# A list scheduler inside the kernel, loads per block of 128 tokens, and one transfer queue

## The chip, the cores and the metric

One core of a Trainium2 chip. The metric is the time of one execution on the device in microseconds, median of the runs in the fast state. Ratios are the mean time of one kernel's fast runs over that of the other's of the same rounds, so they are not quite the ratios of the medians quoted. Spans and times inside an execution come from a profiled run, whose span is 1.7 to 1.9 us shorter than that run's own time.

## The reference

Two stages. The first is a gated linear attention (4 batches, 8 heads, 768 tokens, head size 48), the second a feed-forward layer over 3072 tokens of width 384 with 2048 hidden units:

```python
f = 1 / (1 + exp(-f_logit))
for t in range(S):                                     # per batch and head
    state = f[t][:, None] * state + outer(k[t], v[t])  # 48 x 48
    y[t]  = q[t] @ state
x = y as (3072, 384)
h = x @ w_in                                           # 384 x 2048
out = softplus(h) @ w_out                              # 2048 x 384
```

## The kernel before

The tokens are cut into 24 blocks of 128. For each block the attention turns the recurrence into matmuls (cumulated log gates `cs`, transposes `qkT`, scores `pp`, state `uu`, output `oo`, transpose back `xTp`). The feed-forward layer is `f1` (48 matmuls a block into `hh`, then exp and log on ScalarE) and `f2` (16 matmuls a block into `ops`). A fixed plan sets the order: attention of a block runs 40 steps ahead of its first `f1`, and `f2` 30 steps behind `f1`.

```python
    def load(name, t, b, hold=False):                   # one batch (6 blocks) of one tensor
        sb = work.tile([128, H, NC, 64], FP32, name=name, tag=name, bufs=2)
        ...
        nc.sync.dma_start(out=sb.rearrange("p h c d -> p (h c) d")[:, :, 0:D],
                          in_=t[b].rearrange("h (c p) d -> p (h c) d", p=T))
    load("ff", f_logit, 0); load("kk", k, 0); load("qq", q, 0); load("vv", v, 0)   # (cut)
    ...
    def load_w_in(w):                                   # GpSimd's queue, cast to bf16 by the DMA
        nc.gpsimd.dma_start(out=w_in_bf[:, :, w * WQ:(w + 1) * WQ], in_=...)
    ...
    for s in range(min(plan), NS + LAG):
        if 0 <= s < NS:
            f1(*divmod(s, NJ))
        for fn, a in plan.get(s, []):                   # attention pieces and loads of this step
            fn(*a)
        if 0 <= s - LAG < NS:
            f2(*divmod(s - LAG, NJ))
```

Of the kernel before, what the change touches and what calls it, by code (L numbers as in the profile page):

```python
# [15 lines left out]
LAG = 30  # L16
LEAD = 40


@with_exitstack  # L20
def kernel(
# [27 lines left out]
    in_t = {}  # L49

    def load(name, t, b, hold=False):
        sb = work.tile([128, H, NC, 64], FP32, name=name, tag=name, bufs=2)
        if hold:
            nc.vector.memset(sb[0:1, 0, 0, 0:1], 0.0)
        nc.sync.dma_start(  # L55
            out=sb.rearrange("p h c d -> p (h c) d")[:, :, 0:D],
            in_=t[b].rearrange("h (c p) d -> p (h c) d", p=T))
        in_t[name, b] = sb

    load("ff", f_logit, 0)  # L60
    load("kk", k, 0)
    load("qq", q, 0)
    load("vv", v, 0)

# [30 lines left out]
    WQ = 512  # L95

    def load_w_in(w):
        nc.gpsimd.dma_start(
            out=w_in_bf[:, :, w * WQ:(w + 1) * WQ],
            in_=moe_w_in[:, w * WQ:(w + 1) * WQ].rearrange("(r p) n -> p r n", p=128))  # L100

    def load_w_out(w):
        nc.gpsimd.dma_start(  # L103
            out=w_out_bf[:, 4 * w:4 * w + 4, :],
            in_=moe_w_out[512 * w:512 * (w + 1), :].rearrange("(j p) n -> p j n", p=128))
# [6 lines left out]
    def emit_bias(w):  # L112
        if w == 0:
            bias_ps[0] = att_bank("biasps")
        for j in range(4 * w, 4 * w + 4):
            nc.tensor.matmul(out=bias_ps[0][:, 0:DM], lhsT=ones, rhs=w_out_bf[:, j, :],
                             start=(j == 0), stop=(j == NJ - 1), skip_group_check=True)
        if w == 3:
            nc.vector.tensor_scalar(out=bias_bc, in0=bias_ps[0][:, 0:DM], scalar1=LN2,
                                    scalar2=None, op0=ALU.mult)  # L120
# [4 lines left out]
    def a_z(i):  # L125
        b, c = divmod(i, NC)
        ft = in_t["ff", b][:, :, c:c + 2, 0:D]
        zt = work.tile([128, 2, H, D], BF16, name="zz", tag="zz", bufs=2)
        nc.scalar.activation(out=ft, in_=ft, func=AF.Exp, bias=0.0, scale=-1.0)  # L129
        nc.scalar.activation(out=zt.rearrange("p c h d -> p h c d"), in_=ft, func=AF.Ln,  # L130
                             bias=1.0, scale=1.0)
        z_t[i], z_t[i + 1] = zt[:, 0], zt[:, 1]

    def a_cs(i):
        ps = att_bank("cs")
        nc.tensor.matmul(out=ps[:, 0:DM], lhsT=negU, rhs=z_t.pop(i).rearrange("p h d -> p (h d)"),  # L136
                         start=True, stop=True, skip_group_check=True)
        cs_ps[i] = ps

    def a_e(i):  # L140
        ps = cs_ps.pop(i)[:, 0:DM].rearrange("p (h d) -> p h d", h=H)
        et = e_bufs[i % 2]
        nc.scalar.activation(out=et[:, H:2 * H, 0:D], in_=ps, func=AF.Exp, bias=0.0, scale=-1.0)  # L143
        nc.scalar.activation(out=et[:, 0:H, 0:D], in_=ps, func=AF.Exp, bias=0.0, scale=1.0)

    def a_mul(i):
        b, c = divmod(i, NC)
        et = e_bufs[i % 2]
        qkp = qkp_bufs[i % 3]
        k_eng = nc.vector if i == 0 else nc.gpsimd  # L150
        k_eng.tensor_tensor(out=qkp[:, H:2 * H, 0:D], in0=in_t["kk", b][:, :, c, 0:D],  # L151
                            in1=et[:, H:2 * H, 0:D], op=ALU.mult)
        nc.gpsimd.tensor_tensor(out=qkp[:, 0:H, 0:D], in0=in_t["qq", b][:, :, c, 0:D],  # L153
                                in1=et[:, 0:H, 0:D], op=ALU.mult)
        if i == 0:
            for w in range(4):
                load_w_in(w)
        vb = work.tile([128, DM], BF16, name="vb", tag="vb", bufs=3)
        nc.gpsimd.tensor_copy(out=vb.rearrange("p (h d) -> p h d", h=H),  # L159
                              in_=in_t["vv", b][:, :, c, 0:D])  # L160
        vb_t[i] = vb
        if i == 1:
            for w in range(4):
                load_w_out(w)

    def a_tr(i):
        qkp = qkp_bufs[i % 3].rearrange("p (a b) d -> p a (b d)", b=2)
        ps = att_bank("qkT", BF16, 1024)
        for a in list(range(NP, 2 * NP)) + list(range(NP)):
            nc.tensor.transpose(ps[:, a * 128:(a + 1) * 128], qkp[:, a, :], ident)  # L170
        qkT = work.tile([128, 2 * NP, 128], BF16, name="qkT", tag="qkT", bufs=2)
        qbd = qbd_bufs[i % 2]
        pv = ps.rearrange("p (a t) -> p a t", t=128)
# [5 lines left out]
    def a_p(i):  # L179
        qkT = qkT_t[i]  # L180
        qbd = qbd_bufs[i % 2]
        pt = work.tile([128, H, 128], BF16, name="ptm", tag="ptm", bufs=2)
        for half in range(2):
            ps = att_bank("pp")
            for u in range(2):
                p = 2 * half + u
                nc.tensor.matmul(out=ps[:, u * 256:(u + 1) * 256], lhsT=qkT[0:112, NP + p, :],  # L187
                                 rhs=qbd[0:112, p, :], start=True, stop=True,
                                 skip_group_check=True)
            nc.vector.tensor_tensor(out=pt[:, 4 * half:4 * half + 4, :],  # L190
                                    in0=ps.rearrange("p (a t) -> p a t", t=128), in1=mask4,
                                    op=ALU.mult)
        ptm_t[i] = pt

    def a_u(i):
        c = i % NC
        if c == NC - 1:
            return
        qkp = qkp_bufs[i % 3].rearrange("p (a b) d -> p a (b d)", b=2)
        ek = e_bufs[i % 2].rearrange("p (a b) d -> p a (b d)", b=2)  # L200
        vb = vb_t[i]
        ps = att_bank("uu")
        for p in range(NP):
            nc.tensor.matmul(out=ps[:, 96 * p:96 * p + 96], lhsT=qkp[:, NP + p, :],  # L204
                             rhs=vb[:, 96 * p:96 * p + 96], start=True, stop=True,
                             skip_group_check=True)
# [3 lines left out]
        so, sn = s_bufs[i % 2], s_bufs[(i + 1) % 2]  # L210
# [3 lines left out]
        nc.vector.tensor_copy(out=ec, in_=ps[:, DM:DM + NP])  # L214
        for lo, e0 in ((0, 0), (64, D)):
            hi = lo + 48
            if c == 0:
                nc.vector.tensor_copy(out=tt[lo:hi], in_=uu[lo:hi, :, e0:e0 + D])
            else:
                nc.vector.tensor_tensor(out=tt[lo:hi], in0=uu[lo:hi, :, e0:e0 + D],  # L220
                                        in1=so[lo:hi, :, e0:e0 + D], op=ALU.add)
        for lo, e0 in ((0, 0), (64, D)):
# [5 lines left out]
    def a_o(i):  # L228
        c = i % NC
# [3 lines left out]
        if c > 0:  # L233
# [11 lines left out]
        xt = work.tile([128, DM], BF16, name="xx", tag="xx", bufs=2)  # L245
        nc.vector.tensor_copy(out=xt, in_=ps[:, 0:DM])  # L246
        x_t[i] = xt

    def a_xt(i):
# [4 lines left out]
        xT = work.tile([128, KT, T], BF16, name="xT", tag="xT", bufs=3)  # L254
        nc.vector.tensor_copy(out=xT, in_=ps[:, 0:DM].rearrange("p (r t) -> p r t", r=KT))
        xT_t[i] = xT


    h_ps, u_t, g_t, o_ps = {}, {}, {}, {}

    def f1(i, j):
        if j == 0:
            g_t[i] = work.tile([128, NJ, T], BF16, name="gg", tag="gg", bufs=4)
        if j % 4 == 0:
            h_ps[0] = psum.tile([128, 4, T], FP32, name="hh", tag="hh", bufs=2)
        if j % 8 == 0:
            u_t[0] = work.tile([128, 8, T], FP32, name="uexp", tag="uexp", bufs=3)
        hp = h_ps[0]
        xT = xT_t[i]
        for r in range(KT):  # L270
            nc.tensor.matmul(out=hp[:, j % 4, :], lhsT=w_in_bf[:, r, j * 128:(j + 1) * 128],  # L271
                             rhs=xT[:, r, :], start=(r == 0), stop=(r == KT - 1),
                             skip_group_check=True)
        if j % 4 == 3:
            a = j % 8 - 3
            nc.scalar.activation(out=u_t[0][:, a:a + 4, :], in_=hp, func=AF.Exp, bias=0.0,  # L276
                                 scale=1.0)
        if j % 8 == 7:
            nc.scalar.activation(out=g_t[i][:, j - 7:j + 1, :], in_=u_t[0], func=AF.Ln,  # L279
                                 bias=0.5, scale=0.5)  # L280

    def f2(i, j):
        if j == 0:
            o_ps[i] = psum.tile([128, 512], FP32, name="ops", tag="ops", bufs=2)
        ps = o_ps[i]
        nc.tensor.matmul(out=ps[:, 0:DM], lhsT=g_t[i][:, j, :], rhs=w_out_bf[:, j, :],  # L286
                         start=(j == 0), stop=(j == NJ - 1), skip_group_check=True)
        if j == NJ - 1:
            osb = work.tile([128, DM], FP32, name="osb", tag="osb", bufs=4)
            nc.vector.tensor_tensor(out=osb, in0=ps[:, 0:DM], in1=bias_bc, op=ALU.add)  # L290
            nc.sync.dma_start(out=out[i * T:(i + 1) * T, :], in_=osb)


    plan = {}

    def at(s, fn, *a):
        plan.setdefault(s, []).append((fn, a))

    for i in range(NB):
        s0 = NJ * i - LEAD  # L300
        if i % 2 == 0:
            at(s0 - 4, a_z, i)
        at(s0, a_cs, i)
        at(s0, a_e, i)
        at(s0 + 2, a_mul, i)
        at(s0 + 10, a_tr, i)
        at(s0 + 12, a_u, i)
        at(s0 + 17, a_p, i)
        at(s0 + 23, a_o, i)
        at(s0 + 27, a_xt, i)  # L310
    for b in range(1, B):
        s0 = 4 if b == 1 else NJ * (NC * (b - 1) - 1) - LEAD + 4
        at(s0, load, "ff", f_logit, b, b == 1)
        at(s0 + 1, load, "kk", k, b)
        at(s0 + 2, load, "qq", q, b)
# [41 lines left out]
```

## Time and profile before

| | before |
|---|---|
| time, median | 231.3 us (fast runs 231.27, 231.50 and, timed later with the changed kernel, 230.50; one slow run of 295.32 left out). The prediction works with 231.5, the figure known when it was written |
| span of the profiled run | 228.5 us (that run took 230.25) |
| TensorE (PE) busy | 182.9 us, 80% |
| ScalarE (ACT), VectorE (DVE), GpSimd (POOL) busy | 63%, 53%, 35% |
| first f1 matmul | 41.5 us |

The busy shares are averages over a start that waits for transfers and a body that TensorE fills. The lines that show the two are in the prediction, with how to read them.

### The profile page before, as it was taken

The numbers are of one execution on the slowest core, as the hardware profiler recorded it, in microseconds if no ns is written. First come the engines' busy times: TensorE is split into PE (matmuls) and PEld (weight loads), VectorE is DVE, ScalarE is ACT, GpSimd is POOL, SyncE is SP. The second block draws the span as 40 slices with busy tenths as digits, with TensorE's granted clock in tenths as the row PEclk, the third lists the DMA queues.
The fourth block names the chain that finished last, engine by engine and source line by source line (L and its number), as shares of the span: only waits on it lengthen the run. The fifth ranks groups of instructions, "written<-read, shape, count | busy, mean of one in ns | idle before, by whom it ended". The sixth has DMA issues, their size and how long they took to land.

```text
span 228.5 us, 5679 instructions
## 1 busy us (share of the span) xinstructions
PE 182.9 (80%) x2368; PEld 148.3 (65%) x2368; DVE 120.3 (53%) x270; ACT 143.3 (63%) x217; POOL 80.2 (35%) x127
## 2 busy tenths in 40 slices
PE   0001127888999299999999999999999999999994
PEld 0000014775887177887778878888788787888872
DVE  7100217665664346664856667666567576665011
ACT  2130014197688069689687897887968879677760
POOL 1000529655133051455223543445143552440000
PEclk9999999999999979999999999999999999999999
DMA  5999999999999999999599799200011000110101
GB/s 111 163 164 163 163 185 167 201 174 168 150 176 166 167 165 168 190 164 214 126 165 158 154 165 185 98 34 35 3 37 39 34 4 34 39 39 34 37 34 69
DMA packets 32026, 27.10 MB, mean 119 GB/s; under 512 B 768, under 2 KB 32000, under 8 KB 32000
## 3 DMA queue, kind: packets, MB, share of 16 engines
q1 hardware_dynamic: 28288, 23.60, 58.9%
q0 software_dynamic: 3712, 3.15, 9.1%
q8 instruction: 18, 0.29, 0.6%
q14 instruction: 8, 0.07, 0.1%
HBM read 25.17 MB, written 4.72 MB: 131 GB/s over the span
## 4 chain that ended last, share of the span: by engine, by line
PE 52%; DMA 19%; SPq 13%; ACT 7%; POOL 4%; DVE 2%; issue 1%; DVEq 0%; POOLq 0%
PE ops L286 21%; PE hh L271 19%; DMA vv<-in_v_dram 14%; SPq L55 13%; DMA out_dram<-osb 5%; PE pp L187 3%; PE qkT L170 3%; ACT zz L130 3%; ACT ff L129 2%; ACT uexp L276 2%; PE cs L136 2%; PE oo L241 1%; POOL w_out_bf L103 1%; PE oo L236 1%; PE uu L204 1%
## 5 line engine op out<-in xcount | busy, mean ns | idle before, releaser
L271 PE MATMUL hh<-xT,w_in_bf 128*128 128x128 bf16 x1152 | 125.6, 221 | 0.5 <-ACT uexp L276 0.5
L286 PE MATMUL ops<-w_out_bf,gg 128*128 128x384 bf16 x384 | 121.1, 328 | 0.0
L271 PEld LDWEIGHTS <-w_in_bf 128*128 128x128 bf16 x1152 | 95.9, 99 | 26.3 <-issue 1.6
L276 ACT ACTIVATE uexp<-hh 128x512 f32<-128x512 f32 x96 | 57.0, 595 | 44.4 <-PE hh L271 44.0
L279 ACT ACTIVATE gg<-uexp 128x1024 bf16<-128x1024 f32 x48 | 50.7, 1057 | 1.5
L190 DVE TENSOR_TENSOR ptm<-pp,mask 128x512 bf16<-128x512 f32 x48 | 30.9, 686 | 20.5 <-PE pp L187 20.4
L286 PEld LDWEIGHTS <-gg 128*128 128x128 bf16 x384 | 37.6, 98 | 5.8 <-issue 3.7
L224 POOL TENSOR_TENSOR sst<-tt,ec 48x192 bf16<-48x192 f32 x40 | 20.1, 503 | 55.1 <-DVE tt L220 45.3
L151 POOL TENSOR_TENSOR qkp<-kk,ee 128x384 bf16<-128x384 f32 x23 | 21.0, 913 | 35.5 <-ACT ee L143 35.3
L174 DVE COPY qkT<-qkT 128x1024 bf16<-128x1024 bf16 x24 | 16.6, 691 | 29.0 <-PE qkT L170 29.0
L153 POOL TENSOR_TENSOR qkp<-qq,ee 128x384 bf16<-128x384 f32 x24 | 21.9, 914 | 23.4 <-DMA qq<-in_q_dram 23.4
L170 PEld LDWEIGHTS <-qkp 128*128 128x128 bf16 x192 | 12.4, 102 | 25.8 <-DVE qkp L151 17.1
L170 PE MATMUL qkT<-ident,qkp 128*128 128x128 bf16 x192 | 16.6, 230 | 13.3 <-POOL qkp L153 7.5
L143 ACT ACTIVATE ee<-cs 128x384 bf16<-128x384 f32 x24 | 11.4, 475 | 22.8 <-PE cs L136 22.8
L290 DVE TENSOR_TENSOR osb<-ops,bias_bc 128x384 f32<-128x384 f32 x24 | 13.4, 558 | 22.2 <-PE ops L286 20.1
L136 PE MATMUL cs<-zz,negU 128*128 128x384 bf16 x24 | 8.5, 352 | 16.0 <-ACT zz L130 16.0
L246 DVE CAST xx<-oo 128x384 bf16<-128x384 f32 x24 | 13.4, 557 | 7.3 <-PE oo L241 6.9
L187 PE MATMUL pp<-qbd,qkT 112*128 112x256 bf16 x96 | 15.4, 284 | 0.5 <-DVE qbd L176 0.5
L129 ACT ACTIVATE ff<-ff 128x768 f32<-128x768 f32 x12 | 10.0, 836 | 8.6 <-DMA ff<-in_f_logit_dram 8.6
L204 PE MATMUL uu<-vb,qkp 128*128 128x96 bf16 x80 | 7.2, 217 | 10.3 <-POOL vb L159 10.3
L159 POOL CAST vb<-vv 128x384 bf16<-128x384 f32 x24 | 12.1, 503 | 8.6 <-DMA vv<-in_v_dram 8.6
L204 PEld LDWEIGHTS <-qkp 128*128 128x128 bf16 x80 | 5.3, 105 | 10.5 <-issue 10.5
(41 smaller groups left out, 149.5 us busy)
## 6 DMA issues: line engine op xcount, KB each, us to landing
out_dram<-osb SPq DMA_DIRECT2D x24, 192.0 KB, 2.3
w_in_bf<-in_moe_w_in_dram POOLq DMA_DIRECT2D x4, 384.0 KB, 9.0
w_out_bf<-in_moe_w_out_dram POOLq DMA_DIRECT2D x4, 384.0 KB, 7.0
ff<-in_f_logit_dram SPq DMA_DIRECT2D x4, 0.2 KB, 10.2
kk<-in_k_dram SPq DMA_DIRECT2D x4, 0.2 KB, 16.0
qq<-in_q_dram SPq DMA_DIRECT2D x4, 0.2 KB, 13.6
vv<-in_v_dram SPq DMA_DIRECT2D x4, 0.2 KB, 16.5
```

Of the source, the lines that this page charges most:

```text
L55: nc.sync.dma_start(out=sb.rearrange("p h c d -> p (h c) d")[:, :, 0:D], in_=t[b].rearrange("h (c p) d -> p (h c) d", p=T))
L151: k_eng.tensor_tensor(out=qkp[:, H:2 * H, 0:D], in0=in_t["kk", b][:, :, c, 0:D], in1=et[:, H:2 * H, 0:D], op=ALU.mult)
L153: nc.gpsimd.tensor_tensor(out=qkp[:, 0:H, 0:D], in0=in_t["qq", b][:, :, c, 0:D], in1=et[:, 0:H, 0:D], op=ALU.mult)
L170: nc.tensor.transpose(ps[:, a * 128:(a + 1) * 128], qkp[:, a, :], ident)
L174: nc.vector.tensor_copy(out=qkT, in_=pv)
L187: nc.tensor.matmul(out=ps[:, u * 256:(u + 1) * 256], lhsT=qkT[0:112, NP + p, :], rhs=qbd[0:112, p, :], start=True, stop=True, skip_group_c ...
L190: nc.vector.tensor_tensor(out=pt[:, 4 * half:4 * half + 4, :], in0=ps.rearrange("p (a t) -> p a t", t=128), in1=mask4, op=ALU.mult)
L224: nc.gpsimd.tensor_tensor(out=sn[lo:hi, :, e0:e0 + D], in0=tt[lo:hi], in1=ec[lo:hi].unsqueeze(2).to_broadcast([48, NP, D]), op=ALU.mult)
L271: nc.tensor.matmul(out=hp[:, j % 4, :], lhsT=w_in_bf[:, r, j * 128:(j + 1) * 128], rhs=xT[:, r, :], start=(r == 0), stop=(r == KT - 1), sk ...
L276: nc.scalar.activation(out=u_t[0][:, a:a + 4, :], in_=hp, func=AF.Exp, bias=0.0, scale=1.0)
L279: nc.scalar.activation(out=g_t[i][:, j - 7:j + 1, :], in_=u_t[0], func=AF.Ln, bias=0.5, scale=0.5)
L286: nc.tensor.matmul(out=ps[:, 0:DM], lhsT=g_t[i][:, j, :], rhs=w_out_bf[:, j, :], start=(j == 0), stop=(j == NJ - 1), skip_group_check=True)
```

## The change

Its intent: block 0 should not wait for a whole batch, the weights should not fight the loads for the DMA, and every engine should get its instructions in an order that a small simulation finds good. The kernel now builds a list of tasks with costs and needs, runs a list scheduler over it on the host, and emits the instructions in the order found. Cut to the core:

```diff
-    def load(name, t, b, hold=False):
-        sb = work.tile([128, H, NC, 64], FP32, name=name, tag=name, bufs=2)
+    def load(n, i):                                     # one block of one tensor
+        t = work.tile([128, H, D], FP32, name=n + n, tag=n + n, bufs=LOADS)      # LOADS = 4
...
-        nc.gpsimd.dma_start(out=w_in_bf[...], in_=moe_w_in[...])
+            t = work.tile([128, KT, WQ], FP32, name="w32", tag="w32", bufs=3)
+            nc.sync.dma_start(out=t, in_=moe_w_in[...])
+        eng = (nc.vector, nc.gpsimd)[a]                 # each casts one half
+        eng.tensor_copy(out=d[:, :, m * a:m * a + m], in_=t[:, :, m * a:m * a + m])
...
+def in_order(tasks, slots):
+    queue = {e: sorted((t for t in tasks if t.engine == e), key=lambda t: t.key) for e in clock}
+    def ready(t):                                       # needs, and the users of the buffer's last turn
+        ...
+    while len(order) < len(tasks):
+        # per engine: the first task by key that can start earliest; over all engines: the earliest
...
+    turn = (blocks(0, 1, 2, 3) + [("wi", w) for w in range(4)] + [("wo", w) for w in range(4)]
+            + blocks(*range(4, NB)))
+    for kd, (n, i) in enumerate(turn):
+        if n in SRC:
+            task(("go", n, i), "SP", 0.5, [(used[n], i - LOADS)], kd, load, (n, i))
+            task(("dma", n, i), "DMA", 1.15, [("go", n, i)], kd)
+            ...
+        else:
+            task(("go", n, i), "SP", 0.5, [], kd, load_w, (n, i), "w32", [("cast", n, i, 1)])
+            task(("dma", n, i), "DMA", 2.45, [("go", n, i)], kd)
+            ...
```

Attention, f1 and f2 keep their instructions; they are split into tasks (`z1`, `z2`, `tr`, `ev`, ...), the lag of f2 becomes 24, and there are more buffers for the block's result (`xT` 6) and the activations (`gg` 6).

## The prediction

> **What bounds the kernel now.** I read three views in this order: the page's 40 slices, the chain of work that ended last, and counts of one matmul line per stretch. The slices say where the time goes:
>
> ```profile
> PE   0001127888999299999999999999999999999994
> DMA  5999999999999999999599799200011000110101
> ```
>
> One slice is 5.7 us. TensorE (PE) does almost nothing for six slices (about 33 us), is near full from the tenth, has one hole (the 2 at slice 14), and is full to the end. The DMA engines are full from slice 2 to 25 and then nearly idle. So the kernel has two parts: a start that waits for transfers, and a body bound by TensorE. The chain names the transfers:
>
> ```profile
> 0.80 0.84 SPq L55
> ...
> 15.27 16.84 DMA vv<-in_v_dram
> 32.17 0.51 POOL vb L159
> ...
> 62.01 16.25 DMA vv<-in_v_dram
> 78.38 0.51 POOL vb L159
> 78.94 0.35 PE uu L204 x4
> ```
>
> Each load moves one whole batch (six blocks of 128 tokens) of one tensor. Block 0 needs only a sixth of each, but waits until v, the fourth, is there at 32.2 us. Batch 1 repeats it: v lands at 78.3. The matmuls in order of time show what that costs:
>
> ```profile
> 74.30 0.33 PE L271 MATMUL hh<-xT,w_in_bf 128*128 128x128 bf16 x3
> 78.94 0.35 PE L204 MATMUL uu<-vb,qkp 128*128 128x96 bf16 x4 [4.31 <-POOL vb L159]
> ...
> 79.23 0.48 PE L286 MATMUL ops<-w_out_bf,gg 128*128 128x384 bf16 x1
> 79.51 0.53 PE L271 MATMUL hh<-xT,w_in_bf 128*128 128x128 bf16 x3
> ```
>
> The bracket is the idle time before the group. TensorE stands for 4.3 us and comes back slower (0.53 us for three matmuls against 0.33).
>
> How fast is the body? Busy time does not say, because matmuls overlap. I count the first feed-forward matmuls (L271, 48 per block); columns are stretch, length, matmul busy (count), weight-load busy (count), clock, DMA share, GB/s:
>
> ```profile
> 41.50:60.00 18.50, 10.31 (x111) 8.18 (x111) 1.00 1.12 177
> 72.00:80.00 8.00, 2.14 (x18) 1.76 (x19) 0.95 1.09 166
> 100.00:120.00 20.00, 13.85 (x126) 10.42 (x126) 1.00 0.89 168
> 120.00:140.00 20.00, 14.60 (x134) 11.23 (x135) 1.00 0.97 160
> 140.00:160.00 20.00, 14.74 (x135) 11.11 (x134) 1.00 0.29 77
> ```
>
> At best 134.5 per 20 us, or 7.14 us a block. The chain's steps give the same: a step of three f1 matmuls and one f2 matmul is 0.33 us, 16 steps are 5.28, and attention adds cumsum 0.165, transposes 0.44, scores 0.43, state 0.28, output 0.38, transpose back 0.165 = 1.86. So TensorE's warm work is 24 x 7.14 + 16 bias matmuls x 0.165 = **174.0 us**. The last matmul ends at 225.1, so 51 us are lost: about 37 before the first f1 at 41.5 (only some 4.3 us of attention was done by then), 6 at the batch-1 hole (4.3 idle plus some 1.8 at half speed), 1.2 in 100 to 120, the other 6 to 7 in 41.5 to 60 (slow clock, and no f2 until w_out is there) and around 85. After the last matmul come 3.4 us (addition, store, end).
>
> **What the Trainium skill says.** "DMA: Bandwidth & Descriptors", section "Issuing engines are not separate DMA queues": transfers from all engines run on the same 16 DMA engines. The trace agrees: loads alone move 163 GB/s, and vv, issued at 15.3, waits for qq and lands at 32.2. Hence one queue costs no bandwidth, and the order is what counts. The same page, "Specifications", wants at least 512 B for full rate. The rows here are 192 B, and stay so on the DRAM side; 163 GB/s agrees. "TensorE: Matmul & The Clock Gate", "Part 1: The HAM clock gate": after a few idle us the array runs at half rate until it has been busy for some 3.4 us. The trace agrees (steps of 0.64 us after the hole, until 82.6). "SBUF — State Buffer", "SBUF: two separate sides": some VectorE copies and GpSimd hold one shared port pair exclusively. That bears on the new casts, done half by each engine; the kernel before has no such pair to show it.
>
> **The change, part by part.** All compute operations stay; the logistic part is cut per block (two of about 0.49 us for each block instead of two of 0.84 for two blocks: 24 x 0.98 - 12 x 1.68 = 3.4 us more on ScalarE, busy 143 of 228 now, so hidden). Added are 16 casts (8 of about 0.8 on VectorE, 8 of about 1.05 on GpSimd, the change's own costs), 6.4 and 8.4 us on engines at 53% and 35%. GpSimd loses 6.2 us of weight issues.
>
> 1. Loads per block. Batch loads land at 10.6, 17.9, 25.2 and 32.2: 7.27 us each, so 1.21 us for a sixth. The sixteen loads of blocks 0 to 3 use the DMA until 0.8 + 16 x 1.21 = 20.2 us; block 0 is complete near 7.5. Attention of four blocks (7.4 us warm, double cold) fits in before the weights.
>
> 2. Weights after them. From 32 to 38 us the trace shows some 205 GB/s, nearly all weights written as bf16, read from twice as many bytes, so a 0.79 MB piece took about 2 us to read; the change's scheduler assumes 2.45, since all bytes are now written too. I take 2.3. The first w_in quarter is moved at 22.5, lands about 1.8 later (the change's figure; a store measures 2.3 from issue to landing), and is cast in 1.05: first f1 at **25.3 us instead of 41.5**. The eight pieces are moved by 20.2 + 18.4 = 38.6, the last cast at 41.5.
>
> 3. Work done by 41.5: attention of four blocks 7.4, f1 of four blocks 4 x 2.64 = 10.6, three quarters of the f2 of block 0 (2.0) and of the bias (2.0): 22.0 us. Lost so far: **19.5 us**, against 37.
>
> 4. From 41.5 until block 4. Its q is moved at 38.6 + 3 x 1.21 = 42.2, lands at 44, and its chain (multiply 0.91, transpose 0.44, copies 1.53, scores and mask 1.5, output 0.38, copy 0.56, transpose 0.17, copy 0.36, seven handovers) takes about 6.3: f1 of block 4 at 50.3. In those 8.8 us TensorE has the rest of f2 for blocks 0 to 3 (8.6), of the bias (0.65) and attention of block 4 (1.86): 11.1 us. So it should stay dense. Thereafter a block takes 4.84 of loads and some 0.6 of store, less than 7.14, so the DMA runs ahead and the batch-1 hole vanishes. I allow 2 us idle in 41.5 to 60, 1 for clock changes, and 2 for places where the set order does not meet real times.
>
> 5. Sum: 174.0 + 19.5 + 2 + 1 + 2 = 198.5 for the last matmul, + 3.4 = 202 span. Before, the timed runs exceed the span by 3.0 us (231.5 against 228.5), the profiled one by 1.75; so **205 us**, a ratio of 0.885.
>
> **The rivals.** (a) The weights are paced by their buffers, not by the DMA. There are three 32-bit buffers for eight pieces; one turn is transfer 2.3 + landing 1.8 + cast 1.05 + issue and first byte about 1.5 = 6.7 us for three, 2.2 each: just on the edge. If the two casts block each other on the shared port (0.8 + 1.05 instead of 1.05), or stand behind attention work, it becomes 2.6 to 3 each and everything after step 2 shifts 3 to 6 us: 208 to 211. For it: the tight sum. Against it: VectorE and GpSimd have little else then.
>
> (b) TensorE starves after the weights: blocks 4 and on come one at a time at 4.84 us, with no stock, and the load of block i waits for the use of block i-4, stores standing in the same issue order behind it. For it: the store that took 10.8 us behind batch loads before. Against it: now at most a few 1.2 us loads lie ahead. It would leave holes in 45 to 65 and slow-clock stretches: 210 to 216.
>
> (c) The static order is wrong on the chip: an in-order engine waits for something the scheduler believed done, and ScalarE (6.06 us per block of 7.14, two PSUM banks between it and TensorE) passes each delay on. The body would run at 7.4 to 7.6 a block: 5 to 10 us more. Against it: the costs in the scheduler are those in the trace (0.165, 0.6, 1.06, 0.91).
>
> (d) The early gain is hidden. It is not, since after the start TensorE is the only bound and its lost time adds directly to the end.
>
> **Range and chances.** The best case (weights at 2 us, no allowances) is about 198; (a) and (b) together about 215. I say 205 us, 199 to 215 in 8 of 10. Faster by over 2% needs anything below 226.9; it would take losses as large as the whole gain to miss that: faster 0.95, same 0.03, slower 0.02.
>
> **What would show it.** In the new profile: f1 starts at 25 to 26 us; PE's slices show some work from the second slice and are near full from the eighth or ninth, without the 2; the four loads of a block land 1.2 us apart; w_out is cast by 41 to 43 us; the L271-like matmul goes at 134 per 20 us from 60 us on; PE's last matmul is at 196 to 202. Wrong would be: a first f1 after 28 us or pieces of weights over 2.6 us apart (a), PE waits for loads after 45 us (b), under 130 f1 matmuls per 20 us in the body (c).

## The result, and the profile after

The changed kernel takes **215.8 us** (215.19 to 216.00, four fast runs), ratio 0.933 (0.930 to 0.937). It is clearly faster, but the gain is 15.5 us where some 26 were predicted, and the time lies just above the range. The page of the changed kernel, slices of 5.35 us:

```profile
span 214.1 us, 5854 instructions
...
PE   0558780019999999999999999999999999999993
...
PEclk9999996557999999999999999999999999999999
DMA  7999999999159976988668755875634111011112
```

The start is as foreseen: TensorE works from the second slice. The last two thirds are full. Between them stand two slices with no work and one with hardly any, the clock falls to half (PEclk, the TensorE clock in tenths) and is not yet back in the slice after, and the DMA is full there, so something late is being loaded. TensorE in order of time (start, length, group; the bracket is idle time and what ended it):

```profile
25.49 1.51 PE L331 MATMUL hh<-xT,w_in_bf 128*128 128x128 bf16 x24 [0.56 <-DVE w_in_bf L163]
...
27.65 2.36 PE L331 MATMUL hh<-xT,w_in_bf 128*128 128x128 bf16 x36 [0.47 <-ACT uexp L339]
...
30.75 0.83 PE L331 MATMUL hh<-xT,w_in_bf 128*128 128x128 bf16 x12
31.42 0.33 PE L316 MATMUL xTp<-ident,xx 128*128 128x128 bf16 x3
47.35 2.74 PE L331 MATMUL hh<-xT,w_in_bf 128*128 128x128 bf16 x24 [15.60 <-DVE w_in_bf L163]
```

The first f1 runs at 25.5 us (25.3 predicted). After 72 f1 matmuls, one and a half blocks' worth, TensorE stands for 15.6 us until the VectorE cast of a w_in piece. The queue on the sync engine (SPq; start, length of the issue, what is loaded) says why that piece is late:

```profile
15.08 0.99 SPq L109 DMA_DIRECT2D vv<-in_v_dram  x1
16.11 2.04 SPq L149 DMA_DIRECT2D w<-in_moe_w_in_dram  x3
18.27 0.83 SPq L109 DMA_DIRECT2D ff<-in_f_logit_dram  x1
19.20 3.34 SPq L109 DMA_DIRECT2D kk<-in_k_dram  x1
22.63 4.54 SPq L109 DMA_DIRECT2D qq<-in_q_dram  x1
27.25 0.64 SPq L109 DMA_DIRECT2D vv<-in_v_dram  x1
...
39.02 0.95 SPq L109 DMA_DIRECT2D vv<-in_v_dram  x1
40.07 0.94 SPq L149 DMA_DIRECT2D w<-in_moe_w_in_dram  x1
41.12 9.25 SPq L154 DMA_DIRECT2D w<-in_moe_w_out_dram  x4
```

Three pieces of w_in are issued at 16.1. The fourth follows at 40.07, behind loads of blocks 4, 5, 6 and 7: sixteen issues stand between 18.27 and 39.97. w_out comes after that. The listed turn has the weights before block 4, but the order on the queue is another one. The casts show the same: the fourth w_in piece is cast from 46.6 us, the last of w_out from 56.3 to 57.5.

The f1 matmuls per stretch (columns as in the prediction):

```profile
35.00:40.00 5.00, 0.00 (x0) 0.00 (x0) 0.50 1.41 188
40.00:45.00 5.00, 0.00 (x0) 0.00 (x0) 0.50 1.19 252
...
120.00:140.00 20.00, 14.85 (x137) 11.30 (x137) 1.00 0.68 143
140.00:160.00 20.00, 15.05 (x138) 11.45 (x137) 1.00 0.61 130
```

The clock is at half in the hole, and the body runs at 137 to 138 per 20 us in the stretches shown (134 to 148 in the others from 80 to 200 us), a little better than the 134.5 of before. The ledger, with the prediction's 174.0 us of warm work, is this. The last matmul ends at 210.8, so 210.8 - 174.0 = 36.8 us of TensorE are lost. By 47.35 it had done 7.4 us of attention and 72 f1 matmuls (24 steps of 0.165 = 4.0), so 36.0 of the 36.8 were lost by then. After the hole little is lost. The ledger hides some of it, because the body is faster than the pace that it assumes: at 137.5 f1 matmuls per 20 us the work would be about 170 us, an estimate, and 4 to 5 us of loss would fall behind the hole, part of it the slow clock.

### The profile page after: what moved, and what is told of

It is laid out like the page before. It is cut to its first block, busy times and chain, and to the rows that moved or that the text cites. A ratio compares the mean times of both kernels' runs of the same rounds, so it can differ in the third digit from the quotient of the medians.

```text
span 214.1 us, 5854 instructions
## 1 busy us (share of the span) xinstructions
PE 182.7 (85%) x2368; PEld 148.7 (69%) x2368; DVE 126.3 (59%) x277; ACT 146.0 (68%) x241; POOL 82.7 (39%) x127
## 4 chain that ended last, share of the span: by engine, by line
PE 74%; DMA 8%; SPq 5%; POOL 3%; DVE 3%; ACT 3%; issue 3%; POOLq 0%
PE ops L351 29%; PE hh L331 28%; SPq L109 5%; PE qkT L224 4%; PE pp L240 4%; DMA w<-in_moe_w_out_dram 3%; DMA w<-in_moe_w_in_dram 3%; DMA ff<-in_f_logit_dram 2%; PE oo L302 2%; PE cs L193 2%; PE xTp L316 2%; PE oo L297 1%; PE uu L257 1%; ACT uexp L339 1%; ACT gg L345 1%
## 5 line engine op out<-in xcount | busy, mean ns | idle before, releaser
L331 PE MATMUL hh<-xT,w_in_bf 128*128 128x128 bf16 x1152 | 115.7, 221 | 16.8 <-DVE w_in_bf L163 16.2
L331 PEld LDWEIGHTS <-w_in_bf 128*128 128x128 bf16 x1152 | 90.2, 99 | 37.9 <-DVE w_in_bf L163 17.3
L351 PE MATMUL ops<-w_out_bf,gg 128*128 128x384 bf16 x384 | 111.9, 326 | 0.0
L351 PEld LDWEIGHTS <-gg 128*128 128x128 bf16 x384 | 37.1, 98 | 5.3 <-issue 0.2
L248 DVE TENSOR_TENSOR ptm<-pp,mask 128x512 bf16<-128x512 f32 x48 | 30.9, 683 | 1.5 <-PE pp L240 1.3
L206 POOL TENSOR_TENSOR qkp<-kk,ee 128x384 bf16<-128x384 f32 x23 | 21.1, 916 | 24.2 <-ACT ee L198 19.9
L224 PEld LDWEIGHTS <-qkp 128*128 128x128 bf16 x192 | 13.3, 105 | 7.5 <-DVE qkp L206 5.6
L224 PE MATMUL qkT<-ident,qkp 128*128 128x128 bf16 x192 | 16.8, 234 | 1.8 <-DVE qkp L206 1.5
L240 PE MATMUL pp<-qbd,qkT 112*128 112x256 bf16 x96 | 16.3, 289 | 2.0 <-DVE qbd L233 1.5
L185 ACT ACTIVATE ff<-ff 128x384 f32<-128x384 f32 x24 | 12.2, 516 | 5.4 <-DMA ff<-in_f_logit_dram 5.4
L163 DVE CAST w_in_bf<-w 128x768 bf16<-128x768 f32 x4 | 3.9, 965 | 15.4 <-DMA w<-in_moe_w_in_dram 15.4
L189 ACT ACTIVATE zz<-ff 128x384 bf16<-128x384 f32 x24 | 12.4, 516 | 0.4
```

What stands on the lines that cost most here:

```text
L206: eng.tensor_tensor(out=qkp_bufs[i % 3][:, H:2 * H, 0:D], in0=in_t.pop(("k", i)), in1=e_bufs[i % 2][:, H:2 * H, 0:D], op=ALU.mult)
L224: nc.tensor.transpose(ps[:, a * 128:(a + 1) * 128], qkp[:, a, :], ident)
L240: nc.tensor.matmul(out=ps[:, u * 256:(u + 1) * 256], lhsT=qkT_t[i][0:112, NP + p, :], rhs=qbd_bufs[i % 2][0:112, p, :], start=True, stop=True,
L248: nc.vector.tensor_tensor(out=ptm_t[i][:, 4 * half:4 * half + 4, :], in0=p_ps.pop((i, half)).rearrange("p (a t) -> p a t", t=128), in1=mas ...
L331: nc.tensor.matmul(out=h_ps[i, j // 4][:, j % 4, :], lhsT=w_in_bf[:, r, j * 128:(j + 1) * 128], rhs=xT_t[i][:, r, :], start=(r == 0), stop ...
L351: nc.tensor.matmul(out=o_ps[i][:, 0:DM], lhsT=g_t[i][:, j, :], rhs=w_out_bf[:, j, :], start=(j == 0), stop=(j == NJ - 1), skip_group_check ...
```

## The experiments

All runs gave correct results. All were timed in rounds with the kernel before, whose median was 230.1 to 230.6; the rounds were on three chips, so a difference of a few tenths between runs of different rounds means nothing.

**Why the scheduler changed the turn.** Theory A: the eight weight pieces share three 32-bit buffers. The issue of the fourth piece has to wait until the first is cast. The scheduler is greedy, so in the meantime it puts the next issues that can go, the loads of blocks 4 to 7, on the sync engine. It believes this harmless, because in its model the DMA is an engine that picks, of all transfers issued, the one first in the turn. Its own clock (the scheduler run alone on the host, no measurement) has f of block 4 issued by 10.0 and moved by 39.9, and the fourth w_in piece issued by 25.5 and landed by 30.9: an overtaking. The same clock ends at 198.9 for this kernel, whose measured span is 214.1. In the traces no weight piece overtook what was issued before it. The sync engine issues in the order written, and "DMA: Bandwidth & Descriptors", section "Queues, rings and completion order", says that each DMA engine takes descriptors in ring order (it does not promise that they complete in that order). The trace agrees: the fourth piece, issued at 40.07, is cast 6.5 us later, and in the run with eight buffers below the pieces are cast in the order of their issue, the last over 13 us after it. Theory B: the casts, which block each other or stand behind attention, make the weights late. Theory C: the loss is in the static order of the body.

**The turn forced on the sync engine** (e1_turn):

```diff
+        prev = [("go",) + turn[kd - 1]] if kd else []
-            task(("go", n, i), "SP", 0.5, [(used[n], i - LOADS)], kd, load, (n, i))
+            task(("go", n, i), "SP", 0.5, [(used[n], i - LOADS)] + prev, kd, load, (n, i))
-            task(("go", n, i), "SP", 0.5, [], kd, load_w, (n, i), "w32", ...)
+            task(("go", n, i), "SP", 0.5, prev, kd, load_w, (n, i), "w32", ...)
```

> The issue of each load is made to follow the one before it in the listed turn, so that the sixteen loads of blocks 4 to 7 no longer stand ahead of the fourth w_in piece and of w_out. The orders on TensorE, GpSimd, VectorE stay as in the changed kernel; ScalarE's differs only in small swaps later on. Theory A (the three 32-bit buffers hold back the last five weight pieces, the scheduler fills the gap with 16 block loads, and the queue is first in first out while the scheduler's DMA is not): the fourth w_in piece is cast by 32 us instead of 47, the last w_out piece by 42 instead of 56.8, TensorE has no hole from 32 to 47, and the time falls by 9 to 13 us, to 203 to 207. Theory B (the two casts block each other or stand behind attention work, so the weights are late whatever the queue does): the pieces stay more than 3 us apart, the last cast comes after 48 us, time 210 to 214. Theory C (the loss lies in the static order of the body): 215 to 216, nothing gained.

Measured: 200.49 us (three fast runs; a fourth, 202.95, was slow), ratio 0.869 (0.866 to 0.872). The weights now go out before block 4:

```profile
16.18 9.25 SPq L149 DMA_DIRECT2D w<-in_moe_w_in_dram  x4
27.21 6.87 SPq L154 DMA_DIRECT2D w<-in_moe_w_out_dram  x4
```

The fourth w_in piece is cast from 31.6 us, the last of w_out from 40.5, and 15.3 us are gone. The orders on TensorE, VectorE and GpSimd are unchanged; ScalarE's differs in small swaps, all late in the body. The next run changes none of them. Theory A expected 203 to 207 and was too cautious; B and C are out as explanations of the main loss.

**Eight weight buffers** (e2_buf8), so that no issue waits for a cast:

```diff
-            t = work.tile([128, KT, WQ], FP32, name="w32", tag="w32", bufs=3)    # and for w_out
+            t = work.tile([128, KT, WQ], FP32, name="w32", tag="w32", bufs=8)
-    slots = dict(..., w32=3, ...)
+    slots = dict(..., w32=8, ...)
```

> Eight 32-bit weight buffers instead of three, nothing else; TensorE's and ScalarE's orders are identical to the changed kernel's. No issue of a weight piece waits for a cast, so the listed turn comes out by itself. Theory A: all eight pieces are issued right behind the sixteenth block load and land about 2.1 us apart, the last by 36 us and cast by 38; time 200 to 205, about 1 to 3 us below the kernel with the forced turn, whose pieces also wait for casts. Theory B: as late as with the forced turn, since the casts and not the buffers would pace the pieces; 210 to 214. Theory C: 215 to 216.

Measured: **198.70 us**, ratio 0.862 (0.860 to 0.864), the fastest kernel. Its sync queue and its slices:

```profile
14.95 0.99 SPq L109 DMA_DIRECT2D vv<-in_v_dram  x1
15.98 3.24 SPq L149 DMA_DIRECT2D w<-in_moe_w_in_dram  x4
19.26 8.31 SPq L154 DMA_DIRECT2D w<-in_moe_w_out_dram  x4
27.69 1.53 SPq L109 DMA_DIRECT2D ff<-in_f_logit_dram  x1
```

```profile
PE   0567898999999999999999999999999999999993
...
DMA  6999999999999899999977755866441101100112
GB/s 126 191 187 216 357 386 374 203 201 166 203 226 219 171 228 170 207 211 193 210 165 152 145 132 129 163 136 133 98 82 41 45 2 43 40 28 16 43 40 80
```

All eight pieces are issued in one go behind the sixteenth block load, they move at over 350 GB/s in slices 5 to 7 and are cast about 2.1 us apart, the last by 39.3 us. TensorE has no hole and is full from slice 8. Its last matmul ends at 193.3, so 19.3 us are lost. Every compute engine has the order of the changed kernel here (the scheduler run on the host gives the same lists), so the 17 us come from the order of the issues alone. The 1.8 us between this and the forced turn are probably what the waits for three buffers cost by themselves; the swaps on ScalarE were not tested apart.

**The loads per block alone** (e5_loads_only): the kernel before with its plan and its weights cast in the DMA, only the loads cut per block.

```diff
-        nc.sync.dma_start(out=sb...[:, :, 0:D], in_=t[b].rearrange("h (c p) d -> p (h c) d", p=T))
+        nc.sync.dma_start(out=d, in_=SRC[name][b, :, c * T:(c + 1) * T, :].rearrange("h p d -> p h d"))
...
+    load_pair(0); load_pair(2)
+    for i in range(4, NB, 2):
+        at(NJ * (i - 3) - LEAD + 3, load_pair, i)
```

> One part alone: the kernel before, with its own fixed plan and its weights cast in the DMA from GpSimd's queue, but with loads per block of 128 tokens (f of two blocks, then k, q, v of each). If the loads per block carry the gain, the wait for v at 32 us and the hole at 74 to 79 us vanish: first f1 at about 20 to 25 us instead of 41.5, w_out there by about 35 us, time 208 to 214, as good as the whole change. If the list scheduler carries it (theory: the fixed plan cannot use the early data), the time stays above 222.

Measured: 212.41 us, ratio 0.921. A few lines of the change are faster than the whole of it. What the rest added as shipped was a loss of 3.4 us, although with the turn mended it adds 13.7.

**The late order with eight buffers** (e6_late8): the place in the queue, or the buffers?

```diff
+            # and eight buffers, as above
+            late = [("go", "v", 7)] if (n, i) not in (("wi", 0), ("wi", 1), ("wi", 2)) else []
-            task(("go", n, i), "SP", 0.5, [], kd, load_w, ...)
+            task(("go", n, i), "SP", 0.5, late, kd, load_w, ...)
```

> Eight weight buffers as in the fast kernel, but the fourth w_in piece and w_out are issued on purpose only after the loads of blocks 4 to 7, the order of the changed kernel. Every engine's order of instructions, the sync engine's too, is then that of the changed kernel, and no piece waits for a buffer. Theory A in its narrow form (what costs is the place of the weights behind sixteen loads in a first-in first-out queue; the three buffers only brought that about): 211 to 215, the fourth w_in piece cast at 44 to 47 us. If the waits for buffers themselves cost: near 199 to 202.

Measured: 215.50 us, ratio 0.934, the time of the changed kernel. Its slices for TensorE and the group after the hole:

```profile
PE   0558990029999999999999999999999999999993
```

```profile
46.52 2.74 PE L331 MATMUL hh<-xT,w_in_bf 128*128 128x128 bf16 x24 [14.20 <-DVE w_in_bf L163]
```

The hole is back (14.2 us) with buffers to spare. Eight buffers do nothing when the weights stand behind sixteen loads. The narrow form of theory A holds.

**The transfers of the change without the list scheduler** (e7_plan_queue): the fixed plan, loads per block, one queue in the listed turn, eight buffers, casts placed by hand. It also keeps the lag of 30, the smaller result and activation buffers (`xT` 3, `gg` 4) and the logistic part for two blocks at once.

```diff
+    for n in ("wi", "wo"):                # after load_pair(0), load_pair(2)
+        for w in range(4):
+            load_w(n, w)                  # sync queue, 32 bit, eight buffers
...
+        at(4 * w - 1, cast_w, "wi", w)
+        at(16 + 2 * w, cast_w, "wo", w)
```

> Everything of the change but the list scheduler: the fixed plan of the kernel before, loads per block, all transfers in one queue in the turn blocks 0 to 3, w_in, w_out, blocks 4 and on, eight buffers, casts on chip placed in the plan. If the list scheduler's order of the compute engines is worth something beyond the transfers: 204 to 210, against 198.7 with it; the fixed plan puts attention of blocks 2 and 3 behind the first f1 and f2 30 steps behind f1. If only the transfers count: 198 to 201.

Measured: 212.45 us, ratio 0.922, so the scheduler's order, together with the lag and the buffers that came with it, is worth 13.7 us here, more than the 5 to 11 that I expected. How much of it is the order alone was not tested. The waits of TensorE in its first 41 us:

```profile
22.63 1.14 PE L288 MATMUL hh<-xT,w_in_bf 128*128 128x128 bf16 x9 [2.93 <-DVE w_in_bf L125]
...
27.18 0.50 PE L288 MATMUL hh<-xT,w_in_bf 128*128 128x128 bf16 x3 [1.92 <-DVE w_in_bf L125]
...
33.67 1.69 PE L288 MATMUL hh<-xT,w_in_bf 128*128 128x128 bf16 x12 [1.24 <-DVE w_in_bf L125]
...
40.98 0.32 PE L159 MATMUL cs<-zz,negU 128*128 128x384 bf16 x1 [2.12 <-ACT zz L153]
```

It starts f1 at 22.6 us, before the fast kernel's 25.2, but the plan makes it wait for each w_in piece in the middle of block 0, and attention of the following blocks, whose data are there, stands behind. The scheduler lets f1 of blocks 0 and 1 use each piece as it comes.

**Weights cast in the DMA, from GpSimd's queue, under the list scheduler** (e8_castdma):

```diff
-            nc.sync.dma_start(out=t, in_=moe_w_in[...])            # and the 16 casts
+            nc.gpsimd.dma_start(out=w_in_bf[...], in_=moe_w_in[...])
+            task(("go", n, i), "POOL", 0.8, [("mq", 2 if n == "wi" else 3)], ...)
```

> The list scheduler and the loads per block, but the weights are cast in the DMA from GpSimd's own queue as in the kernel before, issued after the q products of blocks 2 and 3; no casts on chip. The two queues share the DMA engines, so w_in does not stand behind loads of blocks 4 to 7. If the single queue with casts on chip is needed for the gain: over 206. If it only matters that the weights are not behind the 16 loads: 198 to 204.

Measured: 202.10 us, ratio 0.877. One queue with casts on chip is 3.4 us better than this (202.1 against 198.7), and only if the order is right. In a queue of their own the weights did not get stuck behind the loads: without weight buffers on chip, TensorE has no hole, only five waits for pieces of weights between 31 and 43 us, 3.4 us in all, the longest 1.71. w_out is issued at 24.2, behind GpSimd's work for block 3; an earlier issue was not tried, so the 3.4 us are not shown to be the queue's own.

Together, medians in us:

| | weights cast by the DMA, own queue | one queue in the listed turn, cast on chip |
|---|---|---|
| fixed plan and its buffers, loads per block | 212.4 | 212.5 |
| list scheduler and its buffers, loads per block | 202.1 | 198.7 (215.8 as shipped) |

**Weights after three blocks** (e9_three), a candidate for something better:

```diff
-    turn = (blocks(0, 1, 2, 3) + ... + blocks(*range(4, NB)))
+    turn = (blocks(0, 1, 2) + ... + blocks(*range(3, NB)))       # costs 1.05 and 2.1, turn forced
```

> The candidate: eight buffers, forced turn, and the weights after three blocks instead of four (transfer costs in the scheduler set to the measured 1.05 and 2.1 us). First f1 about 4 us earlier, at 21 us, but only three blocks of work in stock while w_out lands: 196 to 198.5, 0 to 2.5 us under the kernel with eight buffers. If the body and not the start holds the rest: the same 198.7.

Measured: 199.57 us, ratio 0.865 (0.862 to 0.867, overlapping the 0.860 to 0.864 of four blocks). A miss: no gain. f1 does start at 19.4 us, 6 us earlier than with four blocks, but its last matmul ends at 194.2 instead of 193.3. TensorE had four waits of 0.3 to 0.8 us for casts between 19 and 29 us and a thinner stretch between 60 and 80 (18.9 us busy of 20). The start saved is given back, probably because less work is in stock when the weights have taken the queue; the forced turn and the new costs changed along with the three blocks and were not tested apart.

**Late weights that the scheduler knows of** (e10_known), to part the late data from the wrong belief:

```diff
+    turn = (blocks(0, 1, 2, 3) + [("wi", w) for w in range(3)] + blocks(4, 5, 6, 7)
+            + [("wi", 3)] + [("wo", w) for w in range(4)] + blocks(*range(8, NB)))
+    # turn forced, eight weight buffers, costs 1.05 and 2.1, five exponential buffers (uexp)
```

> The late order of the transfers again (blocks 0 to 3, three w_in pieces, blocks 4 to 7, then the fourth piece and w_out), but now written in the turn, so that the scheduler reckons with it, with transfer costs of 1.05 and 2.1 us. (It needs five exponential buffers instead of three, or its own slots lock.) Attention of blocks 4 and 5 and more of f1 can then fill the hole from 32 to 47 us. If the loss came from the engines' orders being made for weights that were believed to be there: 203 to 209, most of the loss won back. If late weights cost as such, whatever the orders: 211 to 215.

Measured: 209.73 us, ratio 0.911, between the two expectations. TensorE still waits, but less; it is the longest of its waits:

```profile
48.37 1.46 PE L331 MATMUL hh<-xT,w_in_bf 128*128 128x128 bf16 x12 [5.63 <-DVE w_in_bf L163]
```

So of the 16.8 us between the late order (215.5) and the right one (198.7), about 5.8 came from engine orders made for weights that were believed to be there, and about 11 from the late weights as such. The split holds for this schedule, not as a law; the transfer costs in the scheduler differed too, and they have no control.

**Its control** (e12_late8_u5), since that run had two more exponential buffers:

```diff
# the late order with eight weight buffers, and:
-            u_t[i, a // 2] = work.tile([128, 8, T], FP32, name="uexp", tag="uexp", bufs=3)
+            u_t[i, a // 2] = work.tile([128, 8, T], FP32, name="uexp", tag="uexp", bufs=5)
```

> A control for the run in which the scheduler knew of the late weights: late order, eight weight buffers, the engines' orders as in the changed kernel, but with five exponential buffers, as that run had. If the 5.8 us it won came from the orders of the engines: 214 to 216 here, nothing won. If from the two further buffers: near 210.

Measured: 215.62 us, ratio 0.936. The buffers alone give nothing.

**The layout of the load tiles** (e11_padded). I had predicted 1.21 us a load from the batch loads; the trace has issues about 1.04 apart.

```diff
# eight weight buffers, and:
-        t = work.tile([128, H, D], FP32, name=n + n, tag=n + n, bufs=LOADS)
+        t = work.tile([128, H, 64], FP32, name=n + n, tag=n + n, bufs=LOADS)[:, :, 0:D]
```

> The fast kernel with eight buffers, the load tiles padded to 64 columns a head as in the kernel before, so that a partition's line is eight pieces of 192 B at a step of 256 B and not one of 1536 B. If the destination's layout made the loads faster than predicted (1.03 us a load in the changed kernel, 1.21 predicted from the batch loads): loads go back to about 1.2 us, the first w_in piece lands 3 us later, time 200.5 to 203. If the size of a transfer or something else made it: 198.7 as without the padding.

Measured: 203.02 us, ratio 0.882, 4.3 us slower than without the padding, at the upper end of what was expected. TensorE and what the DMA moved, per slice of 5.0 us:

```profile
PE   0477798999999998999999999999999999999993
...
GB/s 120 163 163 163 333 387 373 257 178 159 172 157 212 184 177 192 170 184 205 193 194 202 179 144 170 141 120 160 78 116 44 18 28 42 39 3 39 42 39 78
```

Slices 2 to 4 hold block loads alone: 163 GB/s, exactly as in the batch loads of before, against 191, 187 in the kernel without padding (its GB/s line above). The step on the chip's side of the transfer made the difference in the rate of these loads, not their size: padded, 192 KB and a whole batch go at the same 163 GB/s. The first f1 comes at 26.0 us instead of 25.2, the last weight cast ends at 41.3 instead of 39.3, and at 77 to 78 us (the 8 at the sixteenth slice of TensorE's line) TensorE waits 0.8 us for attention products. The rest of the 4.3 us I did not trace.

## Why the prediction was right or wrong

The direction was right, and so was the shape: TensorE bounds the body, what it loses at the start goes straight to the end, and the hole of batch 1 is gone. The time was wrong by 10.8 us.

The step that failed is number 2, "The eight pieces are moved by 20.2 + 18.4 = 38.6, the last cast at 41.5". It read the listed turn as the order of issue. The runs showed in its place that the scheduler issues sixteen block loads between the third and the fourth piece, so the last cast ends at 57.5. Step 3's loss of 19.5 us by 41.5 became 36.0 by 47.35. In the sum: predicted loss 24.5, measured 36.8, 12.3 more; less 0.1 in the tail (3.3 instead of 3.4), less 1.3 outside the span (1.7 instead of 3.0) = 10.8 (the sum of 205 was rounded). With the turn as it was read, the kernel takes 200.5 us (e1_turn): the failed step is the whole of the miss and more, and the other terms together were 4.5 us too high.

Rival (a) named the right object, three buffers for eight pieces, and the sum showed it on the edge. It was mis-sized, at 3 to 6 us, because it let the queue stand idle while a piece waits (that alone costs about 1.8, e1_turn against e2_buf8). Its 1.5 us for issue and first byte come from no trace. I never asked what a greedy scheduler puts into the gap, and what a first-in first-out queue then does to what comes after. Rival (b) did not happen: after the hole TensorE's only wait in the trace for something loaded is one of 0.4 us for the cast of a w_out piece. Rival (c) was wrong for the body (137 to 138 f1 matmuls per 20 us), but its idea, an engine waiting in a static order for something believed done, is part of it at the start: 5.8 of 16.8 us. Rival (d) was rightly dismissed.

Smaller terms. First f1 at 25.5 us against 25.3, though with two errors that cancel: the loads took 1.04 us and not 1.21 (their layout, as the padded run showed), so the weights were issued from 16.1, but the first piece took 7 us from issue to cast, behind loads still in the queue, and was cast behind attention copies on VectorE. A piece took about 2.1 us, where I took 2.3. Step 4's claim of a dense stretch after the weights holds once the weights are in order: with eight buffers TensorE is full from slice 8. The allowances of 5 us in step 5 for idle, clock and mismatch were not needed there: 19.3 us lost in all.

Three readings in the prediction were loose. The 3.0 us outside the span compare the profiled run (230.25 us) with a median of other runs (231.5); each run here exceeds its own span by 1.7 to 1.9. The line given for one queue costing no bandwidth, v landing behind q, shows two loads of the same queue, so it does not test the claim, and no run here does. And the 163 GB/s put beside the rows of 192 B were in part the padding on the chip's side: with the same rows and no padding the loads went at 187 to 191.

What stays open: the best place of the weights. Three blocks first was no better than four, and I tried no finer mix.

## What to carry to other kernels

A scheduler's model of a queue has to have the queue's discipline: if transfers cannot overtake on the chip, they must not in the model, and a wished turn is only kept if each issue needs the one before it or never has to wait. When an issue can block on a buffer, ask what will be put in front of it; here sixteen harmless loads cost 17 us. Compare the order of issue in the trace with the list in the source before believing either, and try the cheap part of a large change alone, since here it beat the whole.

## What the Trainium skill lacked or had wrong

- "DMA: Bandwidth & Descriptors" has small descriptors as the cause of slow transfers ("Why small descriptors are slow (HBM only)"), and I found no figure in it for the step on the SBUF side. "Perfetto Trace Analysis", "Contiguity and DMAs", has a sentence that contiguity counts within a partition's line, also without a figure; the runs agree with it. With rows of 192 B in DRAM in both cases, lines of 1536 B in a partition went at 187 to 191 GB/s (e2_buf8), and eight pieces of 192 B at a step of 256 B at 163 GB/s (e11_padded, and the kernel before).
- The same page, "Issuing engines are not separate DMA queues", calls the time to initiate a DMA usually small relative to the DMA. Here it is not once other transfers are in flight. The sync engine's issue of a 192 KB load takes 0.43 us for the first, 0.9 to 1.1 us for the later ones, all the time of its transfer, and 3.3 to 4.5 us behind three weight pieces (changed kernel, 0.74, 19.20 and 22.63 us); that of a batch load takes 0.84 for the first and 5.5 to 6.8 for those behind it (kernel before). It looks as if an engine that issues into a full queue is held. No page gives such times.
- "SBUF — State Buffer", "SBUF: two separate sides", has VectorE and GpSimd lock a shared port pair for a whole instruction, and the second one fully blocked. The trace agrees in part. In the kernel with eight buffers GpSimd's cast of half a w_out piece takes 0.83 us when it starts first and 1.22 when VectorE's cast of the other half, which takes 0.56, has just started:

```profile
31.38 0.83 POOL L163 CAST w_out_bf<-w 128x768 bf16<-128x768 f32 x1 [1.27 <-DMA w<-in_moe_w_out_dram]
...
33.49 1.22 POOL L163 CAST w_out_bf<-w 128x768 bf16<-128x768 f32 x1 [1.28 <-DMA w<-in_moe_w_out_dram]
```

```profile
33.46 0.56 DVE L163 CAST w_out_bf<-w 128x768 bf16<-128x768 f32 x1 [0.84 <-DMA w<-in_moe_w_out_dram]
```

The page gives no such durations. Two halves side by side on these engines are not a cast in the time of one half. But the second is not held to the other's end in full: here GpSimd takes 0.39 us more where VectorE had 0.53 still to run, and a w_in piece, cast at 24.4 us in 1.03, takes only 0.20 more where VectorE had 0.60 (spans on GpSimd are rough in these profiles).
